# Copying num out of PSUM at once in the second batch, and forming x's two parts from the copy

## The chip, the cores and the metric

The kernel runs on one core of a Trainium2 chip. The metric is the time of one execution in device microseconds (us). Five engines run beside each other: TensorE (PE) multiplies matrices, VectorE (DVE) and ScalarE (ACT) do elementwise work and reductions, GpSimd (POOL) a little more of it, SyncE (SP) issues DMAs. PE writes its results to PSUM, from which only DVE and ACT can fetch them here.

## The reference

Eight batches of linear attention with random features, and behind them a gated two-layer product (a * b, then out). All arrays are fp32.

```python
# attention: 8 batches, 8 heads, 576 rows, head size 64, 128 features
def phi(x):
    proj = np.einsum('bhsd,md->bhsm', x, omega)
    sq = np.sum(x * x, axis=-1, keepdims=True) / 2.0
    h = proj - sq
    h = h - np.max(h, axis=-1, keepdims=True)
    return np.exp(h) / np.sqrt(m)
q_p, k_p = phi(q_s), phi(k_s)              # q and k, scaled
kv = np.einsum('bhsm,bhsd->bhmd', k_p, v)
z = np.sum(k_p, axis=2)
num = np.einsum('bhsm,bhmd->bhsd', q_p, kv)
den = np.einsum('bhsm,bhm->bhs', q_p, z)[..., None] + 1e-06
attn_out = num / den
# x: the 4608 rows of attn_out, 512 wide; d_ff = 1536
a = x @ w_a
b = x @ w_b
return a * b @ w_out
```

## The kernel before

A batch is four head pairs (hp 0 to 3, two heads each). For a head pair the kernel multiplies keys and queries with omega (`four`, L508: `ppk` and `ppq`, sixteen products in a block that alternate between the two), forms the features (`hk`, `hq`) with ACT's exponentials, sums keys times values (`kv_burst`, L750, `pkv`), turns the key-value matrix and the features round through DRAM (`qdr`, read back into `hq`, one slice of it copied as `kl`), divides by the denominator (`hq<-hq,dn`), and multiplies (`num`, L818, `pm`: 64x512 twice). num's result is a quarter of x for that batch, transposed. `num` is queued in `pending` and goes out with the next `kv_burst`, right behind `pkv` on PE; the last rows (the tail) go into the spare columns of `pkv` (L820) and are copied as `xts`, the key-value matrix as `k`.

Every fp32 operand of the gated product is used as two parts of a reduced form, fp32r: a high part and what is left. `split` (L452) forms the two parts of x: a cast (`copier`, L329, on ACT) and a subtraction (`subber`, L337, on DVE). Both read num in PSUM. A product is then three matmuls: high by high, high by low, low by high.

The gated product of batch b runs between the attention of batch b+1. For the first two batches it is plain: `pa` and `pb` (L1147) for twelve column groups, `a` out of PSUM, the product `ghl` and its parts, and `o` (L957) with the weights `wo`, four output tiles that are copied to `osb` (two buffers) and sent out. From the third batch on a scheme with fewer products is used (L1239 `p`, sums on DVE at L1249 and L1299), and `sums` copies num of two head pairs to SBUF, in the two buffers of the ring `xf`.

PSUM is divided in rings. The ring "at" has two banks, for `ppk`, `ppq`, `pkv` and `pm`. So a block of feature products behind num must wait until `pkv` has been read by `xts` and `k`, and until `pm` has been read by both steps of `split`.

The order on every engine is made by a planner in the same file. Each step names the engines it may use with a cost, the buffers it needs, a priority and a margin. `schedule` lays the steps out by these costs: PE takes them by readiness and priority, and DVE, ACT and POOL by due times, which are derived from the plan before. Four plans are made and the shortest by these costs is put out. A step that is added in one place can therefore change the order and the choice of engine far from it. SP's queue, which issues nearly all transfers, is laid out in the same plan.

## Time and profile before

| | |
|---|---|
| median of the runs (lowest to highest) | 1063.24 us (1061.07 to 1063.3) |
| the profiled execution | 1063.66 us |
| its span, first to last instruction | 1061.9 us |
| its mean granted TensorE clock | 0.998 |
| PE busy | 1044.9 us, 98% |
| DVE busy | 891.0 us, 84% |
| ACT busy | 593.3 us, 56% |
| POOL busy | 106.2 us, 10% |

PE's busy share leaves 17 us of the span; DVE's and ACT's waits count only where PE waits for them. In the rows further down an entry [idle <-releaser] says how long the engine stood still in front of an instruction, and what ended that.

### The profile page before, as it was taken

The page shows a single profiled execution, that of the slowest core. Times are in us where ns is not written, and L with a number is a line of the kernel's source. Part 1 is how long each engine was busy: PE and PEld are TensorE (multiplying, and loading weights), DVE is VectorE, ACT ScalarE, POOL GpSimd, SP SyncE. Part 2 cuts the span into 40 slices and gives each one's busy share as a digit, 9 for nine tenths or more (in the row PEclk, how much of TensorE's full clock was granted, in tenths as well). Part 3 has the DMA queues.
Part 4 walks back from the last instruction along what each step waited for, and adds up shares of the span by engine and source line. Part 5 has one row for each costly group of instructions (what it writes and reads, how often), then busy time and mean ns, then how long its engine had stood idle before and what let it go on. Part 6 is the DMA issues. An engine that isn't in the chain of part 4 may idle for free.

```text
span 1061.9 us, 22058 instructions
## 1 busy us (share of the span) xinstructions
PE 1044.9 (98%) x7806; PEld 921.1 (87%) x7806; DVE 891.0 (84%) x2228; ACT 593.3 (56%) x1640; POOL 106.2 (10%) x177
## 2 busy tenths in 40 slices
PE   9999999999999999999999999999999999999997
PEld 7878777777789888988989889889889989999997
DVE  6999999799997789779777878878877677998766
ACT  7897788677775655665454656555554123232211
POOL 0121111111111111111011111111110000000000
PEclk9999999999999999999999999999999999999999
DMA  9777887899899898988989998988878889999981
GB/s 355 262 239 262 286 274 263 287 323 327 290 321 370 284 294 299 352 286 316 302 297 312 299 311 292 340 279 288 280 279 266 268 302 318 322 324 345 353 316 51
DMA packets 123646, 314.16 MB, mean 296 GB/s; under 512 B 17680, under 2 KB 40976, under 8 KB 123536
## 3 DMA queue, kind: packets, MB, share of 16 engines
q1 hardware_dynamic: 122656, 312.10, 85.9%
q8 instruction: 61, 1.00, 0.4%
q10 hardware_dynamic: 880, 0.66, 0.2%
q14 instruction: 49, 0.40, 0.1%
HBM read 255.52 MB, written 57.18 MB: 294 GB/s over the span
## 4 chain that ended last, share of the span: by engine, by line
PE 81%; DVE 12%; DMA 3%; ACT 2%; issue 1%; SPq 0%; DVEq 0%; ACTq 0%
PE p L1239 39%; PE o L957 18%; PE o_P L1027 5%; PE ppk L508 4%; PE pa L1147 3%; PE pkv L750 3%; PE pb L1147 3%; PE pm L818 2%; DVE sm L531 1%; DMA out_dram<-osb 1%; DVE zero L769 1%; PE ppq L508 1%; ACT hq L779 1%; DMA raw<-in_wab_dram 1%; PE p L1027 1%
## 5 line engine op out<-in xcount | busy, mean ns | idle before, releaser
L1249 DVE TENSOR_TENSOR c<-p,c 128x512 f32<-128x512 f32 (+1 forms) x336 | 207.5, 618 | 83.4 <-PE p L1239 78.8
L957 PE MATMUL o<-wo,ghl 128*128 128x512 f32 x1008 | 268.4, 396 | 0.0
L957 PEld LDWEIGHTS o<-wo,ghl 128*128 128x128 f32 x1008 | 176.6, 188 | 30.8 <-issue 0.2
L1239 PE MATMUL p<-Sa,t 128*128 128x256 f32 x1008 | 143.6, 281 | 0.0
L1239 PEld LDWEIGHTS p<-Sa,t 128*128 128x128 f32 x1008 | 132.3, 188 | 4.9
L703 POOL TENSOR_TENSOR z<-hk 128x256 f32<-128x256 f32 x56 | 45.2, 807 | 666.3 <-ACT hk L544 438.3
L779 ACT ACTIVATE hq<-hq,dn 128x128 f32<-128x128 f32 x224 | 69.8, 393 | 29.7 <-DVE dn L775 28.0
L329 ACT COPY c<-p 128x256 f32<-128x256 f32 x84 | 31.1, 370 | 97.7 <-PE p L1239 89.2
L508 PE MATMUL ppk<-om,X 64*128 64x128 f32 x504 | 75.0, 288 | 4.6 <-ACT k L329 2.3
L508 PEld LDWEIGHTS ppk<-om,X 64*128 64x128 f32 x504 | 62.1, 190 | 18.7 <-ACT k L329 2.8
L1147 PE MATMUL pa<-x,wa 128*128 128x512 f32 x288 | 75.6, 403 | 1.7 <-DVE x L337 1.7
L769 DVE CUSTOM_DVE_ANT_0 zero<-hq,zb 128x128 bf16<-128x128 f32 x224 | 72.7, 324 | 3.6
L508 PE MATMUL ppq<-om,X 64*128 64x128 f32 x504 | 73.4, 287 | 1.5 <-DVE x L337 0.9
L1239 PE MATMUL p<-Sb,t 128*128 128x256 f32 x504 | 74.6, 284 | 0.0
L1147 PE MATMUL pb<-x,wb 128*128 128x512 f32 x288 | 74.4, 401 | 0.0
L1239 PEld LDWEIGHTS p<-x,t 128*128 128x128 f32 x504 | 69.0, 188 | 6.1 <-ACT oc L329 0.9
L544 ACT ACTIVATE hq<-hq,sm 128x128 f32<-128x128 f32 x192 | 63.5, 395 | 19.3 <-DVE sm L539 18.9
L1239 PE MATMUL p<-x,t 128*128 128x256 f32 x504 | 73.5, 281 | 0.7 <-ACT oc L329 0.7
L1239 PE MATMUL p<-Sb,bq 128*128 128x256 f32 x504 | 74.1, 283 | 0.0
L329 ACT CAST ghl<-c 128x512 fp32r<-128x512 f32 (+1 forms) x67 | 37.1, 573 | 58.9 <-DVE c L1299 51.4
L1239 PE MATMUL p<-x,wb 128*128 128x256 f32 x504 | 68.9, 283 | 0.6 <-DVE c L1249 0.4
L1239 PE MATMUL p<-x,wa 128*128 128x256 f32 x504 | 68.7, 283 | 0.6 <-DVE c L1249 0.6
(194 smaller groups left out, 2050.4 us busy)
## 6 DMA issues: line engine op xcount, KB each, us to landing
t<-td SPq DMA_DIRECT2D x168, 512.0 KB, 6.0
wo<-wod SPq DMA_DIRECT2D x96, 512.0 KB, 5.5
bq<-bd SPq DMA_DIRECT2D x84, 256.0 KB, 5.6
qdr<-qd SPq DMA_DIRECT2D x112, 160.0 KB, 4.7
hq<-qdr SPq DMA_DIRECT2D x28, 640.0 KB, 6.2
X<-in_kqt_dram SPq DMA_DIRECT2D x30, 512.0 KB, 6.9
raw<-in_wab_dram SPq DMA_DIRECT2D x24, 512.0 KB, 6.8
td<-ts SPq DMA_DIRECT2D x24, 512.0 KB, 6.3
```

The lines of the kernel that those rows point to most:

```text
L329: nc.scalar.copy(o(), i())
L508: nc.tensor.matmul(pps[w].ap[:, c * M:c * M + M], x()[rows, c * P:c * P + P], om.ap[rows], start=True, stop=True)
L544: g.op({"ACT": 392}, lambda e, c=c, w=w, to=to, at=at: nc.scalar.activation(to.ap[:, at + c], src[w](c), AF.Exp, scale=SC, bias=sm.ap[:, 2 ...
L703: g.op({"POOL": pool2(n)}, lambda e: nc.gpsimd.tensor_tensor(o(), a(), c(), op=ALU.add), r=r, w=w, alloc=list(al), prio=pri, deps=zload[-1 ...
L750: nc.tensor.matmul(pkv.ap[D * j:D * j + D, 0:M], vb.ap[:, vc, 0:D], c(), start=(n == 0), stop=(n == 4))
L769: g.op({"DVE": 413}, lambda e, c=c, j=j, rr=rr, qc=qc: nc.vector.tensor_tensor_reduce(out=junk.ap[rr], in0=qc(), in1=zb.ap[rr, j], scale=1 ...
L779: g.op({"ACT": 392}, lambda e, c=c, src=src: nc.scalar.activation(hq.ap[:, c], src(), AF.Copy, scale=dn.ap[:, c:c + 1]), r=[sd, (dn, None) ...
L957: nc.tensor.matmul(po.ap[:], ghl.ap[:, gi, t * P:(t + 1) * P], wo.ap[:, wi], start=(n == 0 and i == 0), stop=(n == NF - 1 and i == 2))
L1027: nc.tensor.matmul(pb.ap[:, t], A[0](ai)[:, t * P:(t + 1) * P], W[0](wi), start=begin and t == j == 0, stop=stop and t == 1 and j == 2)
L1147: nc.tensor.matmul(pb.ap[:], wt.ap[:, wi, c], xs[c].at(xi), start=(c == 0 and i == 0), stop=(c == NC4 - 1 and i == 2))
L1239: nc.tensor.matmul(pb.ap[:, half], wcol(wi, c), xc(xi, c), start=n == 0, stop=n == 5)
L1249: g.op({"DVE": dve(n)}, lambda e: nc.vector.tensor_tensor(c4.ap[:, o], pb.ap[:, half], y(), op=ALU.add), r=[*((pb, k) for k in range(half. ...
```

## The change

`split` gets a branch for batch 1, the second one. There num is first copied from PSUM to SBUF by ACT, as fp32, into a buffer of the ring `xf` (named `xc`). The high part is then cast from this copy, by ACT or by DVE as the planner chooses, and DVE subtracts from the copy as well. The other batches are as before.

```diff
         xt = xmain[b, hp]
         n = HM if xt.half else SM
+        if b == B1 - 1:
+
+            xc, psum, pbuf = g.buf("xf", [P, SM], F32, f"xc_{b}_{hp}"), src, sbuf
+            g.op({"ACT": act(SM)}, copier(lambda: xc.ap[:], psum), r=[pbuf], w=[(xc, None)], alloc=[xc], prio=pri, deps=gate)
+            src, sbuf = (lambda: xc.ap[:]), (xc, None)
+            g.op({"ACT": act(SM), "DVE": 160 + 0.52 * n}, copier(lambda: xt.at(0), src), r=[sbuf], w=[xt.part(0)], alloc=list(al), prio=pri)
+            g.op({"DVE": dve(n)}, subber(lambda: xt.at(1), src, lambda: xt.at(0)), r=[sbuf, xt.part(0)], w=[xt.part(1)], prio=pri)
+            return
         g.op({"ACT": act(n)}, copier(lambda: xt.at(0), lambda: src()[:, 0:n]), r=[sbuf], w=[xt.part(0)], alloc=list(al), prio=pri, deps=gate)
```

The planner makes a new order from it. On PE both orders are the same up to the first num of batch 1 and in the last part of the program; between them they differ in many places. The lines of the changed kernel are 8 higher behind the branch. In all, DVE has 6 more casts of `ghl` and ACT 6 fewer; of the output copies `osb` DVE has 4 instead of 6.

PE at the num of head pair 3 in batch 1 (`pm_3`), before: the four output products of a column group, then `pkv` and `pm_3`, and the block `ppk_10`, `ppq_10` of the next batch directly behind its tail.

```order
L957 MATMUL o_2_982<-wo_2193,ghl_11_2246 128x512 x3
L957 MATMUL o_3_991<-wo_2193,ghl_11_2246 128x512 x3
L750 MATMUL pkv_1_2335<-hk_1_2106,v_0_1757 64x128 x8
L750 MATMUL pkv_1_2335<-htk_1958,v_0_1757 64x128 x2
L818 MATMUL pm_3_2337<-hq_3_1791,kl_2326 64x512 x2
L820 MATMUL pkv_1_2335<-hq_3_1791,kl_2326 64x64 x2
L508 MATMUL ppk_10_2391<-om,X_1_1897 128x128
...
L508 MATMUL ppq_10_2392<-om,X_1_1897 128x128
L1147 MATMUL pa_0_2265<-x_3_2338,wa_600 128x512 x3
L1147 MATMUL pb_0_2286<-x_3_2338,wb_704 128x512 x3
```

The same place of the changed kernel.

```order
L758 MATMUL pkv_1_2309<-hk_1_2075,v_0_1773 64x128 x8
L758 MATMUL pkv_1_2309<-htk_1958,v_0_1773 64x128 x2
L826 MATMUL pm_3_2311<-hq_3_1793,kl_2296 64x512 x2
L828 MATMUL pkv_1_2309<-hq_3_1793,kl_2296 64x64 x2
L965 MATMUL o_0_966<-wo_2273,ghl_11_2254 128x512 x3
L965 MATMUL o_1_972<-wo_2273,ghl_11_2254 128x512 x3
L516 MATMUL ppk_10_2356<-om,X_1_1891 128x128
...
L516 MATMUL ppq_10_2357<-om,X_1_1891 128x128
L1155 MATMUL pa_0_2259<-x_3_2312,wa_600 128x512 x3
L1155 MATMUL pb_0_2287<-x_3_2312,wb_704 128x512 x3
```

`pm_3` comes ahead of all four output products of that column group; two of them stand between num's tail and the block, the other two behind a later block.

ACT at the same num, before: from `kl`, which num reads, to the copy `k` of `pkv` and the next square (`natee`).

```order
L329 COPY kl_2326<-hq_3_1791 128x128
L779 ACTIVATE hq_0_2107<-hq_0_2107,dn_0_2228 128x128 x8
L779 ACTIVATE hq_0_2107<-htq_1959,dn_0_2228 128x128
L725 COPY zq_1_2323<-zq_1_2323 32x8 x3
L329 COPY osb_2_2375<-o_2_982 128x512
L329 CAST x_3_2338<-pm_3_2337 128x512
L329 COPY xts_1522<-pkv_1_2335 128x64
L329 COPY k_2_1_2336<-pkv_1_2335 128x128
```

And in the changed kernel.

```order
L329 COPY kl_2296<-hq_3_1793 128x128
L733 COPY zq_1_2298<-zq_1_2298 32x8 x3
L329 COPY xc_3_2343<-pm_3_2311 128x512
L329 COPY xts_1513<-pkv_1_2309 128x64
L329 COPY k_2_1_2310<-pkv_1_2309 128x128
L329 CAST ts_2353<-tf_2333 128x2x256
L329 CAST ts_2369<-tf_2333 128x2x256
L329 COPY osb_0_2372<-o_0_966 128x512
```

The divides and the output copy no longer stand ahead of what empties the two banks; `xc_3` stands where the cast was, and no cast of `x_3` is in ACT's list.

DVE at the end of batch 2, where the sums of the last column groups (`c_01`) become the parts `ghl_1` and `ghl_0`, before.

```order
L1249 TENSOR_TENSOR c_01_5370<-p_3762,c_01_5370 128x256
L1249 TENSOR_TENSOR c_01_5370<-p_3763,c_01_5370 128x512
L1299 TENSOR_TENSOR c_01_5370<-c_01_5370,c_00_5236 128x512 x2
L337 TENSOR_TENSOR ghl_1_5469<-c_01_5370,ghl_1_5469 128x512
L786 STREAM_TRANSPOSE qd_5480<-hq_1_5148 128x4x288
L337 TENSOR_TENSOR x_0_5444<-pm_0_5443,x_0_5444 128x256
L791 STREAM_TRANSPOSE qd_5480<-k_4_1_5060 128x4x32
L337 TENSOR_TENSOR ghl_0_5501<-c_01_5370,ghl_0_5501 128x512
L1249 TENSOR_TENSOR c_10_5511<-p_3763,c_10_5511 128x2x256
```

And in the changed kernel.

```order
L337 TENSOR_TENSOR x_0_5428<-pm_0_5427,x_0_5428 128x256
L1257 TENSOR_TENSOR c_01_5376<-p_3766,c_01_5376 128x512
L331 COPY osb_2_5489<-o_2_4060 128x512
L1307 TENSOR_TENSOR c_01_5376<-c_01_5376,c_00_5238 128x512 x2
L331 CAST ghl_1_5518<-c_01_5376 128x512
L331 CAST ghl_0_5527<-c_01_5376 128x512
L337 TENSOR_TENSOR ghl_1_5518<-c_01_5376,ghl_1_5518 128x512
L1257 TENSOR_TENSOR c_10_5514<-p_3766,c_10_5514 128x2x256
L337 TENSOR_TENSOR ghl_0_5527<-c_01_5376,ghl_0_5527 128x512
```

The output copy `osb_2`, which is ACT's in the order before, now stands on DVE ahead of the last sums and of the parts of `ghl`; both high parts are cast by DVE as well.

## Rows read from the trace of the kernel before

**Rows 1.** The page, busy time, share of the span and instructions.

```profile
PE 1044.9 (98%) x7806; PEld 921.1 (87%) x7806; DVE 891.0 (84%) x2228; ACT 593.3 (56%) x1640; POOL 106.2 (10%) x177
```

**Rows 2.** Stretches: length, busy by engine (instructions), granted clock, DMA share, GB/s.

```profile
50.00:120.00 70.00, 67.38 (x394) 52.34 (x395) 68.70 (x166) 57.17 (x144) 12.56 (x17) 1.00 0.72 227
180.00:190.00 10.00, 7.55 (x55) 5.22 (x54) 8.15 (x17) 7.14 (x22) 0.00 (x0) 0.87 0.94 339
190.00:200.00 10.00, 10.00 (x53) 8.08 (x53) 7.13 (x15) 7.84 (x22) 3.92 (x6) 0.96 0.97 309
190.00:320.00 130.00, 129.24 (x787) 103.36 (x788) 121.70 (x323) 91.80 (x249) 21.10 (x30) 1.00 0.89 309
```

**Rows 3.** PE's timeline, 183 to 192 us: start, length, engine, line, operation [idle <-releaser].

```profile
183.06 0.28 PE L820 MATMUL pkv<-hq,kl 128*64 128x64 f32 x4
185.64 0.48 PE L508 MATMUL ppk<-om,X 64*128 64x128 f32 x2 [2.30 <-ACT k L329]
186.28 0.37 PE L508 MATMUL ppq<-om,X 64*128 64x128 f32 x1
...
187.36 1.65 PE L1147 MATMUL pa<-x,wa 128*128 128x512 f32 x3
188.81 1.48 PE L1147 MATMUL pb<-x,wb 128*128 128x512 f32 x3
...
191.56 1.67 PE L1147 MATMUL pa<-x,wa 128*128 128x512 f32 x6
```

**Rows 4.** Timeline of ACT and DVE, 181 to 186 us.

```profile
181.00 2.45 ACT L779 ACTIVATE hq<-hq,dn 128x128 f32<-128x128 f32 x8 [0.69 <-DVE dn L775]
...
184.28 0.57 ACT L329 COPY osb<-o 128x512 f32<-128x512 f32 x1
184.76 0.57 ACT L329 CAST x<-pm 128x512 fp32r<-128x512 f32 x1
...
185.34 0.25 ACT L329 COPY k<-pkv 128x128 f32<-128x128 f32 x1
...
185.59 0.64 DVE L337 TENSOR_TENSOR x<-pm,x 128x512 fp32r<-128x512 f32 x1
```

**Rows 5.** PE's timeline, a block of feature products without a stop.

```profile
142.47 0.37 PE L508 MATMUL ppk<-om,X 64*128 64x128 f32 x1
...
143.56 0.73 PE L1147 MATMUL pa<-x,wa 128*128 128x512 f32 x2
```

**Rows 6.** PE's timeline, 113 to 117 us.

```profile
113.26 0.48 PE L508 MATMUL ppk<-om,X 64*128 64x128 f32 x2
114.62 0.37 PE L508 MATMUL ppq<-om,X 64*128 64x128 f32 x1 [0.87 <-DVE x L337]
...
115.71 0.97 PE L1147 MATMUL pb<-x,wb 128*128 128x512 f32 x3
116.52 0.86 PE L957 MATMUL o<-wo,ghl 128*128 128x512 f32 x3
```

**Rows 7.** Groups: instruction xcount | busy us, mean ns | idle before.

```profile
L337 DVE TENSOR_TENSOR x<-pm,x 128x512 fp32r<-128x512 f32 x16 | 10.8, 678 | 0.0
...
L337 DVE TENSOR_TENSOR Sb<-st,Sb 128x512 fp32r<-128x512 f32 x14 | 9.5, 682 | 0.0
...
L331 DVE CAST ghl<-c 128x512 fp32r<-128x512 f32 x19 | 8.2, 429 | 1.2 <-PE o L957 0.5
...
L329 ACT COPY xf<-pm 128x512 f32<-128x512 f32 x12 | 7.1, 590 | 0.0
```

**Rows 8.** The page's DMA issues (KB each, us to landing), then ACT's timeline at 180 us.

```profile
hq<-qdr SPq DMA_DIRECT2D x28, 640.0 KB, 6.2
...
180.01 0.29 ACT L329 COPY kl<-hq 128x128 f32<-128x128 f32 x1
```

**Rows 9.** Waits (us in total, times, longest), then ACT's timeline at 435 us.

```profile
ACT osb L329 <- DMA out_dram<-osb: 13.5, 7, 3.0
...
435.31 0.59 ACT L329 COPY osb<-o 128x512 f32<-128x512 f32 x1 [0.19 <-DMA out_dram<-osb]
```

## Prediction

> **What bounds the kernel now.** I read the page's busy table first: TensorE (PE) is busy for 1044.9 us, 98% of the span, and VectorE (DVE) for 84% [rows 1]. So nothing that merely shortens another engine's work counts. The time can fall only where PE stands still or runs at a lower clock, and it can rise wherever PE is made to wait. Second, the table by stretches: in the two stretches from 180 to 200 us the granted clock averages 0.87 and 0.96 of the full 2.4 GHz (so for part of the time the lower level, 1.2 GHz, was granted) with PE busy for 7.55 of the first 10 us, while from 190 to 320 us taken as a whole it rounds to 1.00 [rows 2]. Third, PE's own timeline there, and the ACT and DVE timeline beside it. The reader should see two spots in batch 1 where PE stops behind num, and I call them place A (head pair 3) and place B (head pair 0).
>
> **Place A.** num and its tail end at 183.34 us (183.06 + 0.28). The feature products ppk and ppq come straight behind and need the two PSUM banks of the same ring. ppk starts at 185.64 after 2.30 us of idling for ACT's copy k, and ppq at 186.28 [rows 3]. ACT was late for three reasons that stand in a row on it: the divides hq<-hq,dn of another head pair from 181.00, an output copy osb at 184.28, and only then x, at 184.76, and k at 185.34. DVE's second part of x ran from 185.59 to 186.23 [rows 4]. What a quiet passage takes: a block of sixteen ppk and ppq products 1.09 us (142.47 to 143.56) [rows 5], a group of three wide matmuls 0.81 us (115.71 to 116.52) [rows 6]. Behind num stand one block, two groups and one block: 2 x 1.09 + 2 x 0.81 = 3.80 us, so pa of the next unit would start at 183.34 + 3.80 = 187.14 us. It starts at 191.56 [rows 3]. Place A loses **4.42 us**: 2.30 of idling, 0.63 in the block with the wait for ppq (1.72 us from its first ppk to pa at 187.36, where 1.09 is usual), and the other 1.49 at the lowered clock (pa to pb takes 1.45 us instead of 0.81).
>
> **Place B.** ppk begins at 113.26, ppq at 114.62 after 0.87 us of waiting for DVE's part of x, and the next group at 115.71 [rows 6]: 2.45 us for a block of 1.09, a loss of **1.36 us**.
>
> **The change, part by part.** It adds, four times, one ACT copy of num from PSUM to SBUF, and the cast and the subtraction then read SBUF. The copy of that shape takes 590 ns, the subtraction takes 678 ns from PSUM and 682 ns from SBUF [rows 7], so no engine has less work: ACT has 4 x 0.59 = 2.4 us more. DVE and ACT are not on the path most of the time, so I cost this at nothing by itself; what hides it is PE's own 98%. If that cover is gone in a passage where ACT is behind, as at A, each copy costs up to its 0.59 us.
>
> What the copy does directly is to free num's bank after one ACT instruction instead of after an ACT cast and a DVE subtraction that stands in DVE's queue. That ends ppq's wait: at A 186.28 becomes about 185.9, at B 114.62 becomes about 113.3 plus ACT. It does not touch k, and k is what ppk waited for at A. The larger part must come from the order of the instructions. The planner puts out another order from num of head pair 0 on. At A, num stands 12 matmuls earlier, and six output products o_0 and o_1 come between it and the block; ACT has kl, zq, the copy, xts and k there, and no divides or osb ahead of k. From num's end, ACT needs copy to k, by the row intervals of x and k (184.76 to the end of k at 185.59) 0.83 us [rows 4]; PE is kept by six products for 2 x 0.81 = 1.62 us. So the stop of 2.30 us goes, ppq's goes, and with no stop I expect the clock to stay up. x's parts come later: cast 0.43 to 0.6 us and subtraction 0.68 us, ready about 0.6 + 0.6 + 0.7 = 1.9 us behind num, plus a DVE queue of some tenths; PE needs them at 1.62 + 1.09 = 2.71 us. What is late next is kl: its row is read back from DRAM (median 6.2 us to land), and it stood at 180.01 [rows 8], 2.2 us before num ran; with num 2.8 us earlier PE may wait for it for 0 to 1.8 us. I take 0.7, nearer the low end, because kl's row carries no wait for its transfer: the data may have been there before ACT came to it. A: -4.42 + 0.7 = **-3.7** (bounds -4.4 and 0).
>
> At B, num stands three matmuls earlier and nine instead of twelve lie between it and the block: 2.4 us by the same pace. On ACT eight divides of hq, their ninth, zq and a weight cast run ahead of the copy, and two squares (natee, natk) fall back behind k. By these I reckon k to be ready 0.6 us after PE gets there, an estimate; ppq's wait goes. B: -1.36 + 0.6 = **-0.7** (bounds -1.4 and +0.3).
>
> At the other two head pairs of batch 1 the block stands 1.4 us behind num instead of 2.8, with 0.83 us needed: nothing, at worst 0.6 each.
>
> The new order reaches far past batch 1. At the end of batch 2, output copy osb_2 moves from ACT to DVE. Output copies wait for the landing of an earlier output's transfer: ACT did so seven times, 13.5 us in all, up to 3.0, and the view has no such row for DVE. In batch 2 one of them, at 435.31, waited 0.19 us [rows 9]. On DVE, osb_2 stands ahead of both ghl casts, and PE's next o needs ghl. I estimate a hold of 1.1 us, of which 0.7 is slack: **+0.4** (bounds 0 and 3.8: 3.0 of hold less 0.7, plus 1.5 us of lowered clock, as at A). Other new short waits, from an order that the trace has not shown: **+0.2** (the bounds are -1 and +3).
>
> Sum: -3.7 - 0.7 + 0.4 + 0.2 = -3.8 us. The profiled execution took 1063.66 us (span 1061.9 and 1.8 around it), so 1059.9; the median of the runs is 0.42 us under the profiled one, hence 1059.5. I say 1059.6.
>
> A rule speaks against the change. The subtraction costs the same from either memory, 678 and 682 ns [rows 7]. The Trainium skill (VectorE: DVE Perf Modes, Rules for kernel authors) says to accept the plain rate from PSUM, or to copy to SBUF first if many operations follow; here two follow. By that rule the copy would bring nothing, and 1063.2 would stand. I hold against it that at A and B it is not the reader's rate that costs but the bank it keeps. The same skill (Perfetto Trace Analysis, Matmuls) wants groups to rotate through banks so that emptying one overlaps the next; ppk's 2.30 us of idling [rows 3] agrees.
>
> **Rivals.** (1) *num waits for kl's round trip instead.* If kl cannot come before 180.0, num waits 1.8 us and a lowered clock takes 1.5 more: 3.3 of A's 4.42 are lost again. Then -1.1 - 0.7 + 0.6 = -1.2: 1062.0. For it: the 6.2 us of the transfer, and kl directly in front of num in the new order. Against: the view of waits has no row in which PE waits for kl.
>
> (2) *osb_2 holds DVE.* At its upper price of 3.8 instead of 0.4, -0.4 remains: 1062.8. For it: seven such waits on ACT. Against: the 0.19 us at 435.31, on the same batch's end [rows 9].
>
> (3) *The copy does not do it.* The copy queues on ACT behind the same work as the cast did, and the banks come free no sooner; the order's gain goes too. 1063.
>
> (4) *Slower: DVE becomes the bound from 190 to 313 us.* DVE is busy for 121.70 of 130 us there, 8.3 idle [rows 2]. If PE gets through A 3.7 us sooner, DVE's reserve shrinks by as much, and the new order hands it six more casts of 0.43 us from ACT and takes osb copies from it, some 1.6 us more. That leaves about 3 of 130, 97.7% busy. From 50 to 120 us DVE is at 68.70 of 70, 98%, and PE idles 2.62 [rows 2]; for 130 us that is 4.9, less the 0.76 that PE idles already, plus 2.1 for one long stop, as A lost beyond its idling: 6.2 us. 1059.6 + 6.2 = 1065.8. It decides from a DVE share of 98% on. For it: the share itself. Against: at its present 94% PE idles for only 0.76 us there.
>
> **How the numbers follow.** A measurement of this kernel can tell 0.2%, 2.1 us: faster is under 1061.1, slower over 1065.4. Forecast 0.53 (1056.5 to 1061.1), rival 1 0.14, rival 2 0.10, rival 3 0.06, rival 4 0.17. A fifth of rival 1 still reaches faster: 0.53 + 0.03 = 0.56. Within 0.2%: 0.11 + 0.10 + 0.06 = 0.27. Slower 0.17. The low end: A and B fully recovered are -5.8 (1057.4) and the other terms at -0.9: 1056.5. The high end stands where rival 4 begins, 1065.4; about 0.17 lies above it and a little below the low end.
>
> **What the profile would show.** Right: num of head pair 3 followed by o_0 and o_1, and the block behind them with less than 0.5 us of idling; granted clock near 1.00 from 180 to 200 us; no ppq waiting for DVE's x in batch 1; ppk at B waiting for k for about 0.6 us. Wrong: PE idle in front of num for kl (rival 1); DVE's osb at about 430 us waiting for a transfer, with PE's o behind it (rival 2); PE waits on DVE between 190 and 313 us that add up to several us (rival 4). What I can least see is the new order in the 600 us behind batch 1: there a wait of 2 us that no row of before shows would undo half of it.

## The result and the profile after

The changed kernel takes 1064.64 us (median of 10 runs, 1063.23 to 1068.24) where the kernel before takes 1061.66 (10 runs, 1059.90 to 1063.30): 1.0029 times, interval 1.0020 to 1.0038. It is **slower by 3.0 us**; 3.8 us faster was forecast. After's profiled execution is the longest of its ten (1068.24 us) and before's (1063.66 us) is longer than any of its ten, so the traces lie 4.6 us apart and the medians 3.0. The forecast of 1059.6 us started from 1063.2, the middle of three executions; over ten, before came out 1.6 us lower. Of r1 and r2 further down, one execution each was disturbed (3548 and 1261 us) and does not enter the ratio.

The page's busy line of after, to be read against [rows 1]: PE has the same 7806 matmuls and is busy for 1.8 us more, DVE for 2.9 us more.

```profile
PE 1046.7 (98%) x7806; PEld 920.4 (86%) x7806; DVE 893.9 (84%) x2233; ACT 592.8 (56%) x1639; POOL 105.1 (10%) x177
```

The stretches of after, against [rows 2] (columns as there). From 180 to 200 us PE now stands still for only 0.34 us, at the full clock. From 210 to 230 there is a hole that before does not have: PE 7.11 of 10 us, and the clock at 0.83 behind it.

```profile
180.00:190.00 10.00, 10.00 (x71) 7.43 (x68) 9.75 (x32) 8.44 (x23) 0.00 (x0) 1.00 0.68 209
190.00:200.00 10.00, 9.66 (x42) 7.55 (x41) 9.36 (x34) 6.74 (x21) 3.67 (x6) 1.00 1.00 337
...
210.00:220.00 10.00, 7.11 (x46) 4.78 (x40) 6.08 (x13) 3.91 (x10) 0.00 (x0) 1.00 0.89 281
220.00:230.00 10.00, 10.00 (x47) 8.10 (x47) 7.89 (x18) 8.00 (x23) 3.99 (x6) 0.83 1.01 406
190.00:320.00 130.00, 125.50 (x731) 99.43 (x730) 118.17 (x312) 86.07 (x235) 20.08 (x30) 0.99 0.89 306
```

Before from 210 to 230 us, columns as above:

```profile
210.00:220.00 10.00, 10.00 (x65) 7.84 (x65) 9.27 (x24) 8.02 (x23) 0.00 (x0) 1.00 0.88 238
220.00:230.00 10.00, 10.00 (x45) 8.20 (x44) 9.93 (x27) 6.76 (x20) 4.77 (x6) 1.00 0.99 375
```

**Place A after**, PE's timeline (start, length, engine, line, operation), against [rows 3]: num at 180.03, the six o, the block between 182.70 and 183.79, pa: no row carries a wait.

```profile
180.03 1.03 PE L826 MATMUL pm<-hq,kl 128*64 128x512 f32 x4
180.89 0.28 PE L828 MATMUL pkv<-hq,kl 128*64 128x64 f32 x4
181.10 1.67 PE L965 MATMUL o<-wo,ghl 128*128 128x512 f32 x6
...
183.79 0.97 PE L1155 MATMUL pa<-x,wa 128*128 128x512 f32 x3
```

**Place B after**, against [rows 6]: ppq's wait for DVE is gone, and ppk waits 1.26 us for the new copy xc on ACT.

```profile
112.80 0.49 PE L516 MATMUL ppk<-om,X 64*128 64x128 f32 x2 [1.26 <-ACT xc L329]
```

**Place D, new**, at 219.5 us, all engines. ACT's cast ts cannot overwrite a buffer whose transfer to DRAM was issued at 208.43; it starts at 216.39 after 4.20 us of waiting. Behind it on ACT stand ghl and the copies hk and hq, which empty the banks that PE's next block wants. PE idles 2.89 us.

```profile
208.43 0.56 SPq L340 DMA_DIRECT2D td<-ts  x1
...
214.29 2.34 PE L965 MATMUL o<-wo,ghl 128*128 128x512 f32 x9
...
216.39 0.62 ACT L329 CAST ts<-tf 128x512 fp32r<-128x512 f32 x1 [4.20 <-DMA td<-ts]
...
218.37 0.62 ACT L329 CAST ghl<-a 128x512 fp32r<-128x512 f32 x1 [1.36 <-DVE a L1163]
218.90 0.58 ACT L329 COPY hk<-ppk 128x512 f32<-128x512 f32 x1
...
219.53 0.49 PE L516 MATMUL ppk<-om,X 64*128 64x128 f32 x2 [2.89 <-ACT hk L329]
```

This is the price of one execution. The kernels q1 and s1 further down have after's order on every engine up to here; in their traces the same cast starts 5.8 and 6.2 us behind the transfer's issue instead of 8.0, after 1.85 and 2.24 us of waiting, and PE stops 0.47 us (q1) and 0.82 us (s1), with no dip of the clock.

```profile
214.49 0.62 ACT L330 CAST ts<-tf 128x512 fp32r<-128x512 f32 x1 [1.85 <-DMA td<-ts]
...
217.63 0.48 PE L517 MATMUL ppk<-om,X 64*128 64x128 f32 x2 [0.47 <-ACT hk L330]
```

```profile
217.47 0.49 PE L517 MATMUL ppk<-om,X 64*128 64x128 f32 x2 [0.82 <-ACT hk L330]
```

Of after's ten executions the two longest have a mean clock of 0.997 and the other eight 0.999 to 1.000. A dip like D's is 1.7 of 1066 us, 0.0016, so it would fit into those two; only one of the ten was traced.

**Place E, new**, at the end of the first column group of batch 2 (DVE and PE, c the sums over the products p). ACT waits for an output's landing before osb, the divides hq come late, DVE's transpose qd waits for them at 320.83 and stands ahead of the third and fourth sum; PE idles 1.43 us for the fourth.

```profile
317.57 0.59 ACT L329 COPY osb<-o 128x512 f32<-128x512 f32 x1 [0.53 <-DMA out_dram<-osb]
...
318.05 2.46 ACT L787 ACTIVATE hq<-hq,dn 128x128 f32<-128x128 f32 x8
...
319.85 0.69 DVE L1257 TENSOR_TENSOR c<-p,c 128x512 f32<-128x512 f32 x1 [0.67 <-PE p L1247]
...
320.83 1.38 DVE L794 STREAM_TRANSPOSE qd<-hq 128x1152 f32<-128x1152 f32 x1 [0.29 <-ACT hq L787]
321.07 0.87 PE L1247 MATMUL p<-x,wa 128*128 128x256 f32 x6
...
322.14 0.38 DVE L1257 TENSOR_TENSOR c<-p,c 128x256 f32<-128x256 f32 x1
...
322.66 0.65 DVE L1257 TENSOR_TENSOR c<-p,c 128x512 f32<-128x512 f32 x1
...
323.37 0.97 PE L1247 MATMUL p<-x,wa 128*128 128x256 f32 x6 [1.43 <-DVE c L1257]
```

**Where the time goes.** To place the difference I took points of the two timelines at which PE has issued exactly the same set of matmuls, and subtracted the start of the next one in before's trace from that in the other's (plus: later than before). The change of this number from one column to the next is what a passage costs or brings; its level also holds what before's own execution lost early on.

```
before's time, us     114-116  163.07  191.56  202.79  222.3  247.63  311.91  333.23  342.36  555.3  785.9
after                   -0.04   +0.68   -3.59   -3.15  +1.76   +1.49   +2.18   +4.28   +5.16  +5.35  +4.61
e1 copy, old order      -0.76   -0.54   +0.19   +0.13  +0.13   +0.13   +0.13   +0.05   +0.05  -0.04  -0.68
e2 new order, no copy   -0.51   +1.89   -2.38   -1.97  -1.01   -1.37   -0.36   +1.59   +2.46  +2.45  +1.46
e3 ts behind            -0.50   +0.44   -3.83   -3.12  -3.13   -2.32   -1.30   +1.70   +2.57  +3.21  +2.72
h1 by hand              -1.15   -1.11   -4.80   -3.24  -0.54   -0.08   +0.23   +0.29   +0.29  +0.34  -0.09
x1 more DVE             -1.18   +0.47   +3.20   +3.13  +3.13   +3.54   +3.54   +3.47   +3.47  +3.33  +3.19
q1 qd behind            -0.11   +1.46   -2.80   -2.61  -1.60   -1.67   -0.35   +2.87   +3.74  +4.03  +3.28
s1 qd and issue         -0.28   +0.71   -3.56   -3.13  -1.77   -2.10   -0.90   +1.07   +1.94  +2.37  +1.84
s2 ts, qd and issue     +0.15   +0.88   -3.39   -3.02  -3.03   -2.56   -1.42   +0.75   +1.62  +2.01  +0.90
n1 cost + 20 ns         -1.94   -1.82   -5.32   -5.31  -5.29   -5.70   -4.28   -4.25   -4.24  -3.52  -3.85
```

(n1 shares no such point with before at 163.07, 247.63 and 555.3; it is taken at 164.44, 249.82 and 553.72.)

In after, A brings 4.3 us (163.07 to 191.56), D takes 4.9 (202.79 to 222.3), and the passage from 312 to 342 us, in which E lies, takes 3.0. The other five traces of the new order (e2, e3, q1, s1, s2) say which of this lasts. A brings 4.3 us in each. The passage from 312 to 342 takes 2.8 to 4.1. D takes 1.0 in e2 and q1 and 1.4 in s1, where it was left as it is in after: the other 3.5 to 3.9 are after's own execution. All six rows also lose 0.7 to 2.4 us between 116 and 163, with the nums of head pairs 1 and 2, where ppk waits for xc (0.34 us at 135.10 in after, 0.76 at 159.65 in q1). Between 191.56 and 311.91, D included, five of them lose 2.0 to 2.7 us, and after 5.8.

### The profile page after: what moved, and what is told of

It is laid out like the page before. It is cut to its first block, busy times and chain, and to the rows that moved or that the text cites. A ratio compares the mean times of both kernels' runs of the same rounds, so it can differ in the third digit from the quotient of the medians.

```text
span 1066.4 us, 22046 instructions
## 1 busy us (share of the span) xinstructions
PE 1046.7 (98%) x7806; PEld 920.4 (86%) x7806; DVE 893.9 (84%) x2233; ACT 592.8 (56%) x1639; POOL 105.1 (10%) x177
## 4 chain that ended last, share of the span: by engine, by line
PE 65%; DVE 2%; DMA 2%; ACT 1%; issue 0%; SPq 0%; DVEq 0%; ACTq 0%
PE p L1247 37%; PE o L965 15%; PE o_P L1035 4%; PE ppk L516 3%; PE pkv L758 2%; DMA out_dram<-osb 2%; PE pm L826 2%; PE p L1035 1%; DVE c L1257 1%; PE ppq L516 1%; PE ppke L516 0%; DVE c L1307 0%; ACT hq L787 0%; ACT hk L329 0%; PE pkv L828 0%
## 5 line engine op out<-in xcount | busy, mean ns | idle before, releaser
L1247 PEld LDWEIGHTS p<-x,wa 128*128 128x128 f32 x504 | 64.9, 188 | 5.8 <-DVE c L1257 2.9
```

The source lines that it names most:

```text
L1247: nc.tensor.matmul(pb.ap[:, half], wcol(wi, c), xc(xi, c), start=n == 0, stop=n == 5)
```

## The experiments

Each ratio is to the kernel before, run on the same chip, with its 95% interval. "Steps moved" are moved in the finished list of steps, so that every other row stays where it was.

**Copy and order apart (e1, e2).** e1 keeps before's order on every engine:

```diff
+ def both(e):                      # one ACT step in place of the cast
+     nc.scalar.copy(xc.ap[:], src())
+     nc.scalar.copy(xt.at(0), xc.ap[:])
+ ... subber reads xc
```

> The copy alone: every engine keeps the order of the kernel before, and only in batch 1 ACT's cast of num becomes a copy and a cast from the copy, with DVE's subtraction reading the copy. Theory 1 (the time was moved by the new order, not by the copy): at the num of head pair 3 k comes 0.59 us later, because the cast now follows the copy ahead of it on ACT, and ppq no longer waits for DVE; together between -0.6 and +0.6 us at each of the two places, in all within 1 us of before, ratio 0.999 to 1.001. Theory 2 (the copy itself costs time, 4 x 0.59 us on an ACT that PE waits for): +2 to +3 us, ratio 1.002 to 1.003. Theory 3 (freeing the bank early is worth something by itself): -2 us, ratio 0.998.

1062.68 us, 1.0007 [0.9998, 1.0016]. The copy alone costs nothing that can be told (at most 1.7 us by the interval) and brings nothing: its row in the table rises by 0.7 us from 163.07 to 191.56, all but 0.1 of it ahead of 170 us, and at A PE stops 2.99 us for ACT's k. e2 keeps after's order and takes the copy out:

```diff
+ nc.scalar.copy(xt.at(0), psum())          # at the copy's place
+ subber(lambda: xt.at(1), psum, lambda: xt.at(0))("DVE")
- ... the later cast and subtraction emit nothing
```

> The order alone: PE, POOL and SP have the order of the changed kernel and so have ACT and DVE but for x in batch 1, where no copy is made: the cast stands in the copy's place and reads PSUM, and DVE's subtraction follows it there and reads PSUM as well. Theory 1 (the order): as slow as the changed kernel, ratio to before 1.002 to 1.004, with the long stop at 219.5 us and the group of stops from 314 to 323 us still there; in batch 1 the block behind num may wait 0.5 us more for DVE. Theory 2 (the copy): 0.999 to 1.001, as before.

1067.14 us, 1.0047 [1.0034, 1.0059]. The order alone is slower than before, by at least as much as the change. In this order the copy may help (1.0029 with it): without it ppk waits for DVE's x at the first three nums of batch 1, 1.59, 1.21 and 0.79 us, where after waits for xc 1.26, 0.34 and less than 0.15 us. But the two intervals overlap, so this is not shown. The long stop of D, which was expected to be still there, is 0.40 us in this trace.

**Place D mended (e3).** Cast, subtraction and store of two ts halves behind hk and hq:

```diff
+ later([ACT ts_101], behind ACT hq_2_2)
+ later([DVE ts_101, SP td_101, DVE tf_11 x3], behind DVE sm_2_2)
+ later([ACT ts_110, DVE ts_110, SP td_110], behind ACT hq_2_2, its next quarter)
```

> The changed kernel, with one thing moved: the weight-sum steps that use the ts buffer whose transfer was still under way (ACT's cast at 216.39 us, which waited 4.20 us, its subtraction, and the tf steps behind it) stand behind ACT's copies of ppk and ppq instead of ahead of them. Theory 1 (that wait held ACT's queue, and through it PE for 2.89 us and one stretch at half clock, 5 us in all): the stop at 219.5 us goes, and the run is 4 to 5.5 us faster than the changed kernel, ratio to before 0.998 to 0.999. Rival (the landing of the transfers sets the pace there, and PE stops a little later for the same time): no change to the changed kernel, ratio 1.002 to 1.004.

1064.35 us, 1.0023 [1.0012, 1.0034]. The stop is gone (-3.12 at 202.79 us, -3.13 at 222.3), which is worth 4.9 us against after's trace; the median falls by 0.3, where 4 to 5.5 were expected. Most of the 4.9 was after's own execution (1.0 to 1.4 in the others), and the moved steps cost something themselves: at 233.64 us ppk now waits 0.50 us for ACT's k. From 222 to 312 us 1.8 us go, from 312 to 342 another 3.9.

**Place A's gain alone (h1, h2, h3).** h1 gives before's kernel what the new order did at A, by hand: two o groups behind num, the divides and an output copy behind k. h2 adds e1's copy.

```diff
+ later([PE o0_2, PE o0_3], behind PE num of head pair 3)
+ later([ACT osb0_2, SP out], behind ACT k)
+ later([ACT nine divides of hq_2_0, zq], behind ACT a1_0)
+ later([DVE osb0_1, SP out], behind DVE x_1_3)
+ later([DVE qd8, zw, qd8, SP zdr0, qdr2], behind DVE ghl1_0)
```

> The kernel before without a copy, in its own order but for place A (num of head pair 3 in batch 1), where the order is changed by hand as the planner changed it: two output products stand behind num instead of ahead of it, and on ACT the nine divides and zq stand behind the copies of the next block, so that x, xts and k follow num at once; DVE's subtraction for x stands ahead of an output copy, and the turn of hq (qd) stands later. Nothing else moves. Theory 1 (the order at A is worth what the trace of the changed kernel gained there, 4.3 us, and the loss lies elsewhere): ppk does not wait, ppq waits up to 0.8 us for DVE's subtraction, no half clock: 3 to 4.5 us faster than before, ratio 0.996 to 0.997. Rival (what A gives is given back behind it, because PE then runs ahead of ACT and DVE): 0.999 to 1.001.

> As the kernel with place A ordered by hand, and with the copy at all four nums of batch 1 (ACT copies, and the cast follows on ACT from the copy). Theory 1 (order matters, the copy hardly): within 0.1% of the same kernel without the copy: ppq's wait at A goes (-0.5 us), k comes 0.59 us later at each num (0 to +0.6). Ratio to before 0.996 to 0.998. Theory 3 (the copy is worth something once the order lets it): 1 us or more under the kernel without the copy, 0.995.

h1 1062.88 us, 1.0012 [1.0004, 1.0021]; h2 1063.32, 1.0015 [1.0006, 1.0024]. The copy makes no difference here that can be told. h1 gains 3.7 us at A (-1.11 to -4.80), as the theory said, and has lost all of it by 247 us, as the rival said. Its trace names the takers: ACT waits for an output's landing, DVE's zq comes late, and PE stops for what hangs on them.

```profile
193.47 0.59 ACT L330 COPY osb<-o 128x512 f32<-128x512 f32 x1 [4.05 <-DMA out_dram<-osb]
...
196.67 3.04 PE L1148 MATMUL pa<-x,wa 128*128 128x512 f32 x12 [1.38 <-ACT a L330]
...
206.41 0.61 ACT L726 COPY zq<-zq 32x8 f32<-32x8 f32 x3 [2.00 <-DVE zq L721]
...
207.39 1.08 PE L819 MATMUL pm<-hq,kl 128*64 128x512 f32 x4 [1.60 <-ACT kl L330]
...
211.35 0.37 PE L509 MATMUL ppk<-om,X 64*128 64x128 f32 x1 [0.48 <-DVE x L338]
...
241.03 0.37 PE L509 MATMUL ppk<-om,X 64*128 64x128 f32 x1 [0.79 <-DVE x L338]
```

h3 is h1 with the first output's transfer issued ahead of two loads on SP: `later([SP natk_2_3, SP v_2_2], behind SP out osb0_1)`.

> The kernel before with place A ordered by hand and no copy, as tried already, but with the output transfer of osb_1 issued ahead of two loads on SP, because in the first hand order it was issued 2.4 us later than before and ACT's next osb waited 4.05 us for its landing at 193.5 us. Theory 4 (the 3.9 us that PE gained at A are given back because DVE's queue and the landings, which run on their own clock, set when the passage up to 241 us ends): the stop at 196.7 us shrinks, but PE meets DVE's subtraction for x at 241 us no earlier; ratio 0.9985 to 1.0005. Rival (the gain was lost only to the late output transfer): 0.9955 to 0.997.

1062.37 us, 1.0005 [0.9996, 1.0014]. The wait for the landing goes (no stop at 196), and the same work stops PE a little later all the same: 1.59 us for kl at 205.00, 1.37 and 0.79 for DVE's x at 209.84 and 239.52 us. h1 and h3 move zq and the turn qd later themselves, so part of what they lose behind A may be the price of these moves; no run separates it.

**How much DVE time is behind A's stop (r1, r2, x1).** In batch 2's eight row sums sq, before's order kept: r1 sums 8 of 64 columns (0.21 us for 0.68 in the traces; 0.13 had been expected), x1 sums twice; r2 is h3 with r1's edit.

```diff
- tensor_reduce(o(), nat.ap[:], ...)
+ tensor_reduce(o(), nat.ap[:, :, 0:8] if b == 2 else nat.ap[:], ...)     # r1, r2
+ for _ in range(2 if b == 2 else 1): tensor_reduce(o(), nat.ap[:], ...)  # x1
```

> The kernel before in its own order, with less work on DVE: eight row sums of squares of batch 2 (sq, between 150 and 223 us) add up 8 of 64 columns only, 0.13 us instead of 0.68 (what is left out cancels in the exponent). Theory 4 (in this order PE and DVE are both full from 190 to 310 us, and PE's stop at A comes from ACT): PE hardly waits for DVE here, so at most the 0.34 us at 241 and some tenths of place A go: ratio 0.998 to 1.000. Rival (DVE sets the time by itself): 3 to 4 us faster, 0.996 to 0.997.

> The kernel before in its own order, with the same eight row sums done twice: 0.6 us more on DVE each, 4.8 us in all between 150 and 223 us. Theory 4 (DVE has no reserve in this passage): most of it comes out at the end, +2.5 to +5 us, ratio 1.0025 to 1.005. Rival (DVE has reserve, PE alone is the bound): under +1 us, ratio up to 1.001.

> Place A ordered by hand with the output transfer first, and the lighter row sums on DVE. Theory 4 (DVE is what takes back the gain at A): now the gain stays: 3 to 4.5 us faster than before, ratio 0.9955 to 0.997, and the lead of PE at 241 us is 2 us or more. Rival (the landings of the transfers take it back, whatever DVE does): as the hand order without this, 0.9985 to 1.0005.

x1 1066.92 us, 1.0053 [1.0041, 1.0065]: DVE, 84% busy in before, is busy for 5.8 us more (896.8 by the page; 4.8 had been expected), and that costs 5.6 us (4.4 to 6.9). In the trace 1.65 us are lost ahead of 163.07 us, where the block behind the num before A now stops for 0.33 us (ppk, for ACT's k) and 0.47 us (ppq, for DVE's x), and 2.7 us at A (+0.47 to +3.20). The stop at A is the same one with a longer price, and the clock's dip is longer too: 0.82 and 0.84 in the two stretches that had 0.87 and 0.96 [rows 2].

```profile
187.78 0.79 PE L512 MATMUL ppk<-om,X 64*128 64x128 f32 x2 [3.98 <-ACT k L329]
189.14 0.58 PE L512 MATMUL ppq<-om,X 64*128 64x128 f32 x1 [0.57 <-DVE x L337]
```

```profile
180.00:190.00 10.00, 5.45 (x45) 3.88 (x46) 9.73 (x26) 6.52 (x20) 0.00 (x0) 0.82 0.81 278
190.00:200.00 10.00, 10.00 (x55) 7.99 (x54) 6.55 (x14) 6.80 (x18) 1.83 (x3) 0.84 1.00 309
```

r1 1060.78 us, 0.9992 [0.9983, 1.0001], r2 1060.54, 0.9989 [0.9980, 0.9998]: some 3.7 us less DVE work (8 x 0.46; 2.8 by r1's page) gives 0.9 us, with an interval that reaches zero, and in r2 1.2 us where 3 to 4.5 were expected. r2 is the only kernel whose interval lies below one, and it leaves work out. r2b is one more execution of r2's kernel, with its trace:

> A second look at place A ordered by hand with the lighter row sums, for its trace. Theory 4 (DVE takes back what PE gains at A): PE's lead on the kernel before, taken from the same starting point at 115 us, is over 2 us at 241 us, where the hand order alone kept 0.2; rival (landings take it back): under 0.7 us.

1062.47 us. From its level at 114.62 us (-1.34) it stands at -5.49 at 196 us and -2.88 at 241, so it keeps 1.5 us there where h1 keeps none; less than theory 4 wanted, more than its rival. At 569 us it stands at -0.08, and all is given back: at 553.95 us PE stops 1.38 us for ACT's hk (0.73 in before), and the clock averages 0.60 from 554 to 558 us.

**A planner told other numbers (n1, n2, k1, k2).** In n1 and n2 no work changes; the planner is told that the cast in batch 1 costs 20 ns more or less, and writes another order.

```diff
- g.op({"ACT": act(n)}, copier(...))
+ g.op({"ACT": act(n) + (20 if b == B1 - 1 else 0)}, copier(...))    # n1; n2: -20
```

> No copy and no change of the work: the kernel before, in which the planner is told that ACT's cast of num in batch 1 costs 20 ns more than it was told. It puts out a new order from it, with about as many rows moved as in the changed kernel. Theory 1 (any new order moves the time by some us, up or down, at random): outside 0.999 to 1.001, with stops in other places than before. Rival (a new order is harmless by itself; what the copy brought into it did the harm): 0.999 to 1.001.

> A second new order without any change of the work: the planner is told that ACT's cast of num in batch 1 costs 20 ns less. Theory 1 (a new order moves the time by some us at random; the first such order came out at 1.0003): outside 0.999 to 1.001. Rival (new orders are harmless, and the changed kernel's is a bad one among them): 0.999 to 1.001.

n1 1062.11 us, 1.0003 [0.9994, 1.0012]; n2 1066.63, 1.0047 [1.0033, 1.0061]. An order drawn anew with no change of work can be as slow as the change, and without one great stop: n2's largest on PE behind the first 60 us are 1.33, 1.01 and 1.01 us.

n1's trace bears on what takes A's gain back. It gains 3.5 us at A too (-1.82 to -5.32), and from 190 to 320 us DVE has more to do than in before (123.78 us, before 121.70):

```profile
190.00:320.00 130.00, 128.88 (x788) 103.25 (x787) 123.78 (x326) 89.01 (x246) 20.11 (x30) 1.00 0.90 314
```

Yet nothing of the gain is lost by 250 us, and 2.5 us of it are left at 311.91. So a nearly full DVE does not take the gain back by itself; it depends on the order. In n1 the rest goes later (-2.37 at 964 us, -1.91 at 1055).

k1 and k2 take the squares out (loads, ACT's squares, DVE's row sums, their small PE sums), from before and from after, and plan anew:

```diff
- sq = row sums of natk**2, natq**2 ; sm bias from sq
+ nc.vector.tensor_scalar(sm.ap[:, 2, :, sl], sm.ap[:, 0, :, sl], -SC, None, op0=ALU.mult)
```

> The kernel before without the squares of q and k altogether: they cancel in the exponent (the bias is the negative maximum), so their loads, ACT's squares, DVE's row sums and the small sums by PE are left out, and the planner makes its own order. Theory 4 (DVE and ACT set the time of the batches up to 310 us and PE sets the rest): PE's 7.5 us of idling up to 320 us mostly go: ratio 0.992 to 0.996. Rival (PE alone is the bound): 0.998 to 1.000.

> The changed kernel (num copied out in batch 1) without the squares, in the order that the planner makes of it. Theory 1 (a copy is worth next to nothing, the order that comes with it decides): within 0.3% of the kernel without squares and without the copy, on either side; ratio to before 0.991 to 0.998. Theory 3 (the copy pays once DVE and ACT have reserve): 0.1 to 0.3% under that kernel.

k1 1067.59 us, 1.0049 [1.0030, 1.0067], although DVE is busy for 844.6 us instead of 891.0; k2 1061.05, 0.9993 [0.9982, 1.0005]. Neither came out as expected. Between two kernels that differ by the copy and by the order lie 6.5 us, and in k1 the order outweighs 46 us less of DVE's time.

**The passage at 312 to 342 us (q1, f1, s1, s2).** q1 puts qd behind the third and fourth sum; f1 takes before's kernel and moves the num that stands at the boundary of the two products there (pkv at 318.46 us, pm at 319.61) behind two products, as in after.

```diff
+ later([DVE qd13, DVE qd13 (k), SP qdr1], behind DVE c2_01 <- p1)              # q1, on after
+ later([PE pkv_3_2 with num, ACT x_3_0, ACT xf_3_0], behind PE p1 <- wa2)      # f1, on before
```

> The changed kernel with one step moved: DVE's turn of hq (1.38 us, at 320.83), which stood between two sums of the gated product of batch 2 and was ahead of the sum at 322.14 for which PE waited 1.43 us at 323.37, stands behind both. Theory 1 (part of the loss is DVE's queue in this passage): the stop at 323 us goes, 1.0 to 1.5 us, ratio to before 1.0012 to 1.002 where the changed kernel has 1.0029. Rival (PE would have waited there for something else): 1.0025 to 1.003.

> The kernel before in its own order, but for one place: in the first units of batch 2's gated product the kv sums and num of batch 3's head pair 0, which stand between the last product of a unit (p<-Sb,bq) and the first of the next (p<-x,wa, at 318 us), stand behind the next two products instead. Theory 6 (a unit boundary without such a filler stops PE for the round trip to DVE's sum c and back, as the changed kernel's at 323 us did): PE then idles 1.0 to 1.5 us in front of the second p<-x,wa, and some 0.5 us more where the next block waits for k; 1 to 2 us slower than before, ratio 1.001 to 1.002. Rival (the stop at 323 us came from DVE's queue in the new order): no stop there, 0.9995 to 1.0005.

q1 1065.52 us, 1.0033 [1.0020, 1.0045]: no gain. f1 1062.06, 1.0003 [0.9993, 1.0013]: without the filling work PE does not wait longer for c (0.33 us at 311.47, 0.42 in before), so its absence is not what makes the stop. It is not free in the trace either: the block behind num now waits for k, and the passage from 311.91 to 333.23 costs 0.8 us.

```profile
322.18 0.37 PE L509 MATMUL ppk<-om,X 64*128 64x128 f32 x1 [0.50 <-ACT k L330]
```

q1's rows (DVE and PE) hold a clue:

```profile
319.56 1.15 DVE L1258 TENSOR_TENSOR c<-p,c 128x256 f32<-128x256 f32 x2 [1.46 <-PE p L1248]
...
320.77 0.97 PE L1248 MATMUL p<-x,wa 128*128 128x256 f32 x6 [1.24 <-DVE c L1258]
```

DVE stood free and waited for PE, and PE then waited for DVE. The list of DVE's waits explains it. The third sum reads the second half of p0; in the new order it is written down behind PE's first group of the next product, which writes p0's first half, and it carries a wait for PE. Three sums of 256 columns carry one in after (at 322.14, 870.87 and 962.95 us).

```
after   c2_01<-p0 128x256 [waits DVE, PE]    c2_01<-p1 128x512 [waits DVE]
before  c2_01<-p0 128x256 [waits DVE]        c2_01<-p1 128x512 [waits DVE, PE]
```

In before none does at this place, but two do later, at 865.88 and 957.99 us, so it is not true that before has none, as the expectation of s1 says. Each of the two, in before as in after, has a stop of PE of 0.3 us behind it:

```profile
865.88 0.42 DVE L1249 TENSOR_TENSOR c<-p,c 128x256 f32<-128x256 f32 x1 [0.63 <-PE p L1239]
...
867.56 0.62 PE L1239 MATMUL p<-x,wa 128*128 128x256 f32 x3 [0.32 <-DVE c L1249]
```

n2's largest stop has the same form: its sum of 256 columns at 310.84 us waits 0.86 us for PE, and at 312.13 PE waits 1.33 us for the sum behind it.

s1 is q1 with the PE step written behind the third sum (no engine's rows move); s2 is s1 with e3's moves.

```diff
+ order.remove(first)                       # PE p0 <- x,wa of the next product
+ order.insert(at("DVE", "c2_01", "p0", 3), first)
```

> The changed kernel with DVE's transpose qd of head pair 1 behind the last two sums of the product that ends at about 321 us (as in the kernel with qd behind), and with one step of the program written earlier: the third of the four sums (the 256-column one, out of p0) is written ahead of PE's first group of the next product, p0 <- x,wa, instead of behind it. No engine's row moves by that, but the third sum, which reads p0, no longer carries a wait for PE; the fourth now carries its own. In the changed kernel three such sums stand behind the next product's first group in the program, in the kernel before none. Theory 8 (the sum was made to wait for a PE group that it does not need, because that group writes another half of the same PSUM tile and was written down first): DVE's third sum starts within 0.2 us of the second's end instead of waiting 1.46 us for PE p, PE's second group of p <- x,wa has no stop (1.24 us with qd behind alone), the passage from 311.9 to 333.2 us of the kernel before grows by 1.0 to 2.0 us instead of 3.2, and the time falls from 1065.5 to 1063.5 to 1064.5. Rival (the passage is short of DVE time or of filling work on PE, whatever the waits): the stop stays within 0.3 us or moves to the next group, the passage still grows by 2.8 us or more, 1065.0 to 1066.

> The kernel just named with the ts steps of batch 2 put behind hk and hq as well, as in the kernel with ts behind (1064.35 us, 1.0023 of the kernel before). Both known faults of the new order are then mended. Theory 8 and the earlier finding that 3.1 us of lead over the kernel before are there at 220 us: no PE stop near 217 and none at 320 us, a lead of -1.3 us at 311.9 that shrinks to between -0.3 and +0.7 at 333.2 (it grew by 3.0 us to +1.70 without the step written earlier), and 1062.0 to 1063.3. Rival (what is won is given back to DVE and the landings in any order): 1063.8 to 1064.6, ratio 1.0020 to 1.0027.

s1 1064.18 us, 1.0018 [1.0009, 1.0027], s2 1063.97, 1.0021 [1.0012, 1.0029]. In s1 the third sum follows the second at once (both in one row), PE's stop at 320 us is gone, and the passage from 311.91 to 333.23 costs 1.97 us instead of 3.22:

```profile
316.81 1.15 DVE L1258 TENSOR_TENSOR c<-p,c 128x512 f32<-128x512 f32 x2 [0.67 <-PE p L1248]
...
318.03 1.93 PE L1248 MATMUL p<-x,wa 128*128 128x256 f32 x12
...
323.00 0.98 PE L1248 MATMUL p<-x,t 128*128 128x256 f32 x6 [0.90 <-DVE c L1258]
```

The wait is shown, and it is a part only: s1 and s2 still pay 2.8 and 3.0 us between 312 and 342 us, of which the stops at DVE's c name 1.1 and 1.3 (in s1 0.62 and 0.90, in s2 0.82 and 0.91, less the 0.42 that before has there). Some of the other 1.7 us shows on the weight loads (PEld), which wait in s1 at four places where before's do not:

```profile
313.67 0.78 PEld L1248 LDWEIGHTS p<-x,wb 128*128 128x128 f32 x6 [0.28 <-DVE c L1258]
...
318.98 0.78 PEld L1248 LDWEIGHTS p<-x,wa 128*128 128x128 f32 x6 [0.19 <-DVE c L1258]
...
342.45 0.78 PEld L1248 LDWEIGHTS p<-Sa,t 128*128 128x128 f32 x6 [0.34 <-ACT c L330]
343.87 0.19 PEld L966 LDWEIGHTS o<-wo,ghl 128*128 128x128 f32 x1 [0.40 <-DVE ghl L338]
```

What each costs PE was not measured. The last two lie between 333.23 and 342.36, which costs 0.9 us in all six traces of the new order. And s2, with D and E mended, is no faster than e3 with D alone: the rival was right on the sum.

## Why the prediction was wrong

**Right: place A and its cause.** The stop and the dip of the clock go, by 4.3 us where 3.7 was forecast, in all six traces of the new order, and the order does it and not the copy, as argued: e1 has the copy and gains nothing at A, h1 has no copy and gains 3.7. num did not wait for kl (rival 1): its row of after at 180.03 carries no wait.

**Wrong: place B, -0.7.** ppk waits 1.26 us for xc, and 1.04 and 1.01 in s1 and s2; 0.6 was the estimate. Against before's trace B brings nothing (after stands at -0.37 us at 110.59 and at -0.04 at 115.71). The work ahead of the copy on ACT is what the prediction lists, but it starts later: the divides wait 1.14 us for DVE's dn, and xc ends at 112.74. Nor was there much to win: in f1, h1, h3, r1, r2b and x1, which leave B as it is in before, the stop of 0.87 us of [rows 6] is gone in three, 0.16 and 0.17 us in two and 0.52 in one. I priced one execution's stop as a lasting one.

**Too low: the other two head pairs of batch 1, "nothing, at worst 0.6 each".** The passage that holds them costs 0.7 to 1.6 us in the five traces with the copy.

**Unfounded: osb_2 on DVE, +0.4.** after's row moves by 0.2 us from 342 to 555, and PE has no stop of 0.25 us between 400 and 500 in after. DVE's osb at 440.63 waits for PE's o (0.67 us), not for a transfer: it costs nothing that shows.

**The step that failed: "Other new short waits, from an order that the trace has not shown: +0.2 (the bounds are -1 and +3)", and with it the sum that keeps A's gain to the end.** From 192 to 342 us the new order loses 4.8 to 6.5 us in five traces and 8.8 in after's, where +0.2 and at most +3 was taken. Two things are in it. First, A's gain does not last behind A. Moved by hand with nothing else changed (h1), A yields 3.7 us, and kl, zq and x collect them within 50 us, in part perhaps because the moves put zq and qd later. DVE's time has a part in this, as far as one trace of each tells: with some 3.7 us less of it (r2b) 2.9 us are lost from 192 to 312 where h3 loses 4.2, and with more of it (x1) the stop at A grows. It is not the whole: n1 has a fuller DVE and loses 1.0 there. The prediction saw that no engine has less work, but took each of PE's stops as lost time that comes back when the stop goes. Second, the new order has stops of its own: D, 1.0 to 1.4 us in three traces and 4.9 in after's, and the passage at 312 to 342, 2.8 to 4.1, of which the wait for PE that the third sum carries is a shown part (1.25 us, q1 against s1). The last paragraph of the prediction had placed such a wait behind batch 1 as what it could least see; it gave it no weight in the sum.

**Rival 4 had the sign, not the cause.** It wanted DVE to be 98% busy from 190 to 313 us. In after DVE is busy for 118.17 of 130 us, 91%, less than the 121.70 of before [rows 2].

**Not the cause: the copy's cost.** 1.0007 in the old order. The Trainium skill (VectorE: DVE Perf Modes, Rules for kernel authors) says to accept the plain rate from PSUM, or to copy first if many operations follow. e1's trace agrees for the two that follow here: DVE's subtraction takes 680 ns from PSUM and 686 from the copy, so the reader gains nothing.

**Open.** What of the 1.7 us in the passage at 312 to 342 us the short waits of the weight loads make, and 1.8 us between 222 and 312 in e3, of which one stop names 0.5. n1 and n2 say that a newly drawn order can differ by as much with no change of work, but not which rows make it.

## What to carry to other kernels

When an edit changes a planned order, hold the order and test the edit alone, then leave the edit out and draw the order anew with a cost changed by nothing that matters: here two such orders came out at 1.0003 and 1.0047, further apart than the edit is from before (1.0029). A stop of the busiest engine need not come back as time when it is removed: price its removal at what the next waits behind it leave, and test that with the order held. A stop in one trace is the price of one execution: 0.87 us at B and 2.89 us at D shrank to 0 to 0.5 and 0.4 to 0.8 in other executions with the same order there. Where a step reads one half of a PSUM tile and another engine's step writes the other half, the order in which the two are written down can make a wait that no engine's own order shows.

## What had not been expected of the hardware

A long stop brought a dip of the clock each time. Worked out from the mean clocks of the stretches (10 us times twice what is missing to 1.00), TensorE ran at the lower level for 3.4 us after 2.30 us of idling in before [rows 2, 3], 3.4 us after 2.89 in after, and 6.8 us around 3.98 in x1. At half speed that is 1.7 us lost besides the idling in each of the first two. In x1 it is less than half of 6.8, because the level had fallen (0.70 from 186 to 187 us) before PE's block began at 187.78. Shorter stops did not do it each time: those of 1.26 and 1.43 us in after left no dip, and one of 1.38 us in r2b stands ahead of one. One ts transfer of 512 KB held its buffer for 8.0 us (208.43 to 216.39) in after and for 5.8 and 6.2 in q1 and s1; the median from issue to landing for td<-ts is 4.1 us on the page of after and 6.3 on that of before.
